# 1,450 products of zeros on TensorE ahead of an attention and feed-forward kernel

## The chip, the cores and the metric

The kernel runs on one core of one Trainium2 chip. The metric is the device time of one execution in microseconds. A core has five engines with queues of their own: TensorE (PE, with its loads of the stationary operand shown apart as PEld), VectorE (DVE), ScalarE (ACT), GpSimd (POOL) and SyncE (SP). Each works through its queue in order; waits between the queues are semaphores, which the framework puts in from the tiles that an instruction reads and writes.

## The reference

Attention in chunks of 32 tokens over 16 tokens to the left, 8 to the right and 8 memory entries, for 4 x 8 heads of 64, and then a feed-forward layer of 512 to 2048 to 512 over all 3,072 tokens:

```python
for c in range(nc):                       # nc = 768 // 32
    q_c = q[:, :, c_start:c_end]
    k_full = np.concatenate([mem_k, k[:, :, l_start:r_end]], axis=2)
    v_full = np.concatenate([mem_v, v[:, :, l_start:r_end]], axis=2)
    scores = scale * np.matmul(q_c, k_full.transpose(0, 1, 3, 2))
    scores = scores - np.max(scores, axis=-1, keepdims=True)
    a = np.exp(scores)
    a = a / (np.sum(a, axis=-1, keepdims=True) + 1e-09)
    out[:, :, c_start:c_end] = np.matmul(a, v_full)
...
h = x @ w_in
g = np.where(h >= 1, h, np.where(h <= -1, 0.0, (h + 1) ** 2 / 4.0))
return (g @ w_out).astype(np.float32)
```

## The kernel before

The 3,072 tokens are cut into 6 blocks of 512 (TB). A block's attention is made in two halves of 256 tokens: scores on TensorE (pe_scores, first_attention), maximum, difference and sum on VectorE, the exponential on ScalarE, transposition, and the product with the values (pe_values). Its result goes into the tiles xth and xtl: every float32 operand of the feed-forward layer is kept as a high part of the type float32r and a low part, the rest.

The feed-forward layer has 16 steps a block (NFC), one for each 128 of the 2048 columns. In a step pe_hidden makes 12 products of 128x128 by 128x512 into the tile ps_h (high by high, low by high, high by low, for four pieces of 128 rows), ScalarE and VectorE work out the gate and its parts gh and gl, and pe_out makes 12 more into the four banks of ps_o. In 96 steps these are 2,304 products of full size, less what the early steps do in halves of 256 columns.

The weights come from memory in 16 pieces w_0 to w_15 of 8,192 bytes a partition. Each piece is turned in place into its high and low part by decode: one pass on ScalarE, three on VectorE, one on ScalarE, one on VectorE. Decodes, the attention of the first three blocks and the first 32 feed-forward steps are interleaved by the list FIRST, in which a name stands for the next part of its chain and "+" for the next load of the list early. After it the loop over s goes on step by step.

Every engine's instructions are kept in the order of the program (the class InOrder). So VectorE and ScalarE can't pass a step that waits for TensorE, and SP can't issue a load ahead of one that waits. SP's first loads are, in this order: query and key tiles 0 and 1 (first_qk), value tile 0 (first_v), w_0, value tile 1, query tile 2, w_1, query tile 3, value tiles 2 and 3, w_2 and so on.

At the start stand the memset of the tile warm on VectorE, keep_warm(8), which is eight products of warm with itself that nobody reads, and make_identity, which writes ident on GpSimd. Then the list begins with the scores of the first attention (g0).

Memory: the pool const has ident (512 bytes a partition) and the 16 weight tags; xpool, apool and gpool follow. In order of first use const's tags are ident, w_0, w_13 (borrowed first by query tile 2), w_1, w_14 (query tile 3), w_15 (value tiles 2 and 3), w_2, w_3, w_4, w_5 and the rest. Query tiles 0 and 1 and value tiles 0 and 1 are in apool. Together the tiles of all pools take about 222 KB of a partition. All operands of the large products start at multiples of 512 bytes from one another: the pieces of the weights and of xth and xtl by their sizes, gh and gl through the 128 bytes of the tile "offset" ahead of them.

Of the kernel before, what the change touches and what calls it, by code (L numbers as in the profile page):

```python
# [8 lines left out]
F32 = mybir.dt.float32  # L9
F32R = mybir.dt.float32r  # L10
# [6 lines left out]
P = 128  # L17
# [34 lines left out]
LAST = 2  # L52


class InOrder:


# [3 lines left out]
    def __getattr__(self, name):  # L61
        def call(*args, **kwargs):
            return self.tc.keep_in_program_order(getattr(self.engine, name)(*args, **kwargs))  # L63

        return call


@with_exitstack
def attn_ffn_kernel(ctx: ExitStack, tc: tile.TileContext, first_qk, first_v, qk, vw, w, out):
    nc = tc.nc  # L70
    engines = (nc.tensor, nc.scalar, nc.vector, nc.gpsimd, nc.sync)
    pe, act, dve, pool, sp = (InOrder(tc, e) for e in engines)
# [8 lines left out]
    SEQ = 24  # L81
    SCALE = 1.0 / float(D) ** 0.5
    n2 = 2 * DM

    const = ctx.enter_context(tc.tile_pool(name="const", bufs=1))
    xpool = ctx.enter_context(tc.tile_pool(name="xpool", bufs=2))
# [43 lines left out]
    place = {key: divmod(n, 2) for n, key in enumerate(weight_order(NFC))}  # L130
# [421 lines left out]
    for name in FIRST.split():  # L552
# [4 lines left out]
        if name not in chains:  # L557
            kind, i = name[0], int(name[1:])
# [15 lines left out]
    for s in range(first * NFC, steps):  # L574
# [30 lines left out]
        else:  # L605
            n, i = LAST // LAG, s - first * NFC
# [11 lines left out]
def weight_order(n):  # L618

    order = [(0, 0), (0, 1)]  # L620
    for fc in range(2, n):
        order += [(0, fc), (1, fc - 2)]
    return order + [(1, n - 2), (1, n - 1)]
# [81 lines left out]
```

## Time and profile before

| | us |
|---|---|
| median of 2 runs | 599.89 |
| lowest, highest | 599.82, 599.96 |
| the profiled execution | 600.11 |
| its span, first to last instruction | 598.3 |
| ScalarE busy | 280.3 |
| VectorE busy | 325.6 |

The profile is that of one execution. "Busy" is the union of an engine's instructions; for TensorE the ends are modelled, so that consecutive products overlap in the rows and their spacing has to be read from starts. The mean granted clock of TensorE over the span is 0.999 of full speed. In rows of the timeline the first number is the start in us from the first instruction, the second how long the merged instructions last, "x8" their number, and the bracket the idle time of the engine before them with what ended it. In rows of groups the numbers behind the bar are busy time in us, mean duration of one in ns, and idle time before.

### The profile page before, as it was taken

How to read it: one execution, taken by the hardware profiler on the slowest of the kernel's cores; microseconds unless marked ns; L12 is line 12 of the kernel's file. 1: busy time of each engine (PE TensorE's matmuls, PEld its weight loads, DVE VectorE, ACT ScalarE, POOL GpSimd, SP SyncE). 2: the span in 40 equal slices, each digit the busy share in tenths (PEclk: the TensorE clock that was granted, in tenths of full speed). 3: DMA queues.
4: the chain of work that ended last, by engine and by line, in shares of the span. 5: the costliest groups of instructions: out<-in, count | busy, mean ns of one | idle time of the engine just before them, and what ended most of it. 6: DMA issues, size and time to landing. Idle time of an engine off the chain costs nothing.

```text
span 598.3 us, 12265 instructions
## 1 busy us (share of the span) xinstructions
PE 582.7 (97%) x5496; PEld 483.5 (81%) x5496; DVE 325.6 (54%) x466; ACT 280.3 (47%) x503; POOL 0.7 (0%) x6
## 2 busy tenths in 40 slices
PE   5899999999999999999999999999999999999996
PEld 2888888788888888888888888888888888888885
DVE  5999999986474224636423644623564632322222
ACT  2689864554435335444435443434443444543442
POOL 0000000000000000000000000000000000000000
PEclk9999999999999999999999999999999999999999
DMA  8999300424051004012101223200310000100001
GB/s 355 422 418 419 148 1 0 178 82 168 1 177 71 0 1 158 26 65 108 71 1 71 107 71 107 71 1 34 144 71 2 1 2 0 71 0 1 0 1 70
DMA packets 9844, 55.31 MB, mean 92 GB/s; under 512 B 1088, under 2 KB 1088, under 8 KB 5184
## 3 DMA queue, kind: packets, MB, share of 16 engines
q1 hardware_dynamic: 9792, 54.53, 23.6%
q8 instruction: 43, 0.70, 0.5%
q14 instruction: 9, 0.07, 0.0%
HBM read 48.23 MB, written 6.29 MB: 91 GB/s over the span
## 4 chain that ended last, share of the span: by engine, by line
PE 82%; DVE 15%; issue 2%; DMA 1%; ACT 0%; DVEq 0%; ACTq 0%
PE ps_o L63 38%; PE ps_h L63 38%; DVE f L63 6%; PE ps_x L63 3%; DVE wr L63 2%; PE ps_s L63 2%; DVE gw L63 1%; DVE gl L63 1%; DVE pr L63 1%; DVE den L63 1%; DMA qk<-in_first_qk_dram 1%; DVE pt L63 1%; DVE mx L63 1%; DVE xtl L63 0%; DVE rin L63 0%
## 5 line engine op out<-in xcount | busy, mean ns | idle before, releaser
L63 PE MATMUL ps_h<-xth,wr 128*128 128x512 f32 (+1 forms) x832 | 195.6, 377 | 1.1 <-DVE wr L63 1.1
L63 PE MATMUL ps_o<-wr,gh 128*128 128x512 f32 x768 | 194.7, 390 | 0.0
L63 PEld LDWEIGHTS ps_h<-xth,wr 128*128 128x128 f32 x832 | 149.0, 190 | 30.3 <-DVE wr L63 1.5
L63 PEld LDWEIGHTS ps_o<-wr,gh 128*128 128x128 f32 x768 | 143.3, 188 | 29.4
L63 DVE SCALAR_TENSOR_TENSOR gw<-gw,gt 128x512 f32<-128x512 f32 (+1 forms) x104 | 67.2, 649 | 164.9 <-ACT gw L63 164.6
L63 ACT ACTIVATE gw<-ps_h 128x512 f32<-128x512 f32 (+1 forms) x104 | 58.6, 563 | 159.0 <-PE ps_h L63 158.9
L63 PE MATMUL ps_o<-wr,gl 128*128 128x512 f32 x384 | 106.9, 389 | 0.0
L63 PE MATMUL ps_h<-xtl,wr 128*128 128x512 f32 (+1 forms) x416 | 104.8, 374 | 0.0
L63 DVE TENSOR_TENSOR gl<-gw,gh 128x512 fp32r<-128x512 f32 (+1 forms) x104 | 67.4, 649 | 65.8 <-ACT gh L63 65.7
L63 ACT CAST gh<-gw 128x512 fp32r<-128x512 f32 (+1 forms) x104 | 61.1, 590 | 69.9 <-DVE gw L63 69.9
L63 PEld LDWEIGHTS ps_h<-xtl,wr 128*128 128x128 f32 x416 | 75.3, 190 | 13.9
L63 PEld LDWEIGHTS ps_o<-wr,gl 128*128 128x128 f32 x384 | 72.1, 188 | 15.1
L63 ACT ACTIVATE gw<-gw 128x512 f32<-128x512 f32 (+1 forms) x104 | 62.4, 600 | 0.0
L63 ACT ACTIVATE gt<-ps_h 128x512 f32<-128x512 f32 (+1 forms) x104 | 58.3, 561 | 0.0
L63 DVE STREAM_TRANSPOSE pt<-pr 32x512 f32<-32x512 f32 (+1 forms) x60 | 41.2, 698 | 1.3
L63 DVE SCALAR_TENSOR_TENSOR f<-w,f 128x1024 uint32<-128x1024 uint32 x32 | 39.0, 1220 | 0.4
L63 ACT ACTIVATE pr<-pr 128x1024 f32<-128x1024 f32 (+1 forms) x14 | 13.1, 937 | 35.1 <-DVE pr L63 35.0
L63 PEld LDWEIGHTS ps_x<-pt,v 64*64 64x64 f32 x1536 | 25.1, 142 | 5.0 <-issue 3.3
L63 PE MATMUL ps_x<-pt,v 64*64 64x32 f32 x1536 | 26.6, 226 | 1.2 <-ACT pt L63 1.2
L63 ACT CAST xth<-ps_x 128x512 fp32r<-128x512 f32 x24 | 13.1, 591 | 20.6 <-PE ps_x L63 20.6
L63 ACT CAST wr<-f 128x1024 fp32r<-128x1024 f32 x16 | 16.8, 1051 | 11.7 <-DVE f L63 11.7
L63 PEld LDWEIGHTS ps_s<-qk 64*32 64x32 f32 x1536 | 17.1, 112 | 6.1 <-issue 3.1
(27 smaller groups left out, 182.6 us busy)
## 6 DMA issues: line engine op xcount, KB each, us to landing
w<-in_w_dram SPq DMA_DIRECT2D x16, 1024.0 KB, 19.8
qk<-in_qk_dram SPq DMA_DIRECT2D x10, 1536.0 KB, 6.5
v<-in_vw_dram SPq DMA_DIRECT2D x10, 1024.0 KB, 5.5
out_dram<-ob SPq DMA_DIRECT2D x24, 256.0 KB, 2.0
qk<-in_first_qk_dram SPq DMA_DIRECT2D x4, 768.0 KB, 8.7
v<-in_first_v_dram SPq DMA_DIRECT2D x4, 512.0 KB, 12.7
```

Of the source, the lines that this page charges most:

```text
L63: return self.tc.keep_in_program_order(getattr(self.engine, name)(*args, **kwargs))
```

## The change

Ahead of all pools a tile of zeros is made, 128 partitions by two halves of 8,704 float32r words (69,632 bytes a partition), and filled by one memset on VectorE (the half for stationary operands) and one on GpSimd (the half for moving operands). Then pe_zeros issues 1,450 products, all into two banks of PSUM that nothing reads, and both pools are closed. The main part of the kernel is as it was.

The products are 30 alike, with both operands at the beginning of their halves, and then ten each of 142 kinds by the list that ahead gives: (place in bytes, step of the stationary columns in words, moving operand as one run or as runs of so many words at such a step, moving columns, stationary columns). In that order: 64 places 4 bytes apart; steps 2, 4, 8, 16, 32, 62, 64 and 66 at four places each; six patterns of the moving operand in which every second run is skipped, with steps 16 and 64 of the stationary one, at two places each; one such pattern with a stationary operand in one run, at two places; 128, 256 and 384 moving columns at four places each; 32 and 64 stationary columns at four places each.

```diff
+REPEAT = 10
+
+
+def ahead():
+
+    todo = [(4 * n, 1, 1, 512, 128) for n in range(64)]
+    todo += [(r, k, 1, 512, 128) for k in (2, 4, 8, 16, 32, 62, 64, 66) for r in (0, 16, 64, 128)]
+    for run, step in ((1, 2), (2, 4), (4, 8), (8, 16), (16, 32), (32, 64)):
+        todo += [(4 * run * r, k, (run, step), 512, 128) for k in (16, 64) for r in (0, 1)]
+    todo += [(r, 1, (32, 64), 512, 128) for r in (0, 128)]
+    todo += [(r, 1, 1, n, 128) for n in (128, 256, 384) for r in (0, 64, 128, 192)]
+    todo += [(r, 1, 1, 512, n) for n in (32, 64) for r in (0, 64, 128, 192)]
+    return todo
...
+def pe_zeros(pe, to, zeros):
+
+    fixed, moving = zeros[:, 0], zeros[:, 1]
+    for _ in range(3 * REPEAT):
+        ps = to.tile([P, 512], F32, name="ps_z")
+        pe.matmul(ps, fixed[:, 0:P], moving[:, 0:512], start=True, stop=True)
+    for place, step, kind, n, m in ahead():
+        c = place // 4
+        a = fixed[:, c : c + (m - 1) * step + 1 : step]
+        if kind == 1:
+            b = moving[:, 0:n]
+        else:
+            run, k = kind
+            b = moving[:, 0 : n // run * k].rearrange("p (b q) -> p b q", q=k)[:, :, 0:run]
+        ps = to.tile([P, 512], F32, name="ps_z")
+        for _ in range(REPEAT):
+            pe.matmul(ps[0:m, 0:n], a, b, start=True, stop=True)
...
+    with tc.tile_pool(name="ahead", bufs=1) as at, tc.tile_pool(name="ps_a", bufs=2, space=bass.MemoryType.PSUM) as to:
+        zeros = at.tile([P, 2, 8192 + 512], F32R, name="zeros")
+        dve.memset(zeros[:, 0].bitcast(F32), 0.0)
+        pool.memset(zeros[:, 1].bitcast(F32), 0.0)
+        pe_zeros(pe, to, zeros)
```

## The prediction

> **What bounds the kernel now.** I read the page first (busy time, the slices, the chain that ended last), then the timeline of the first 40 us, the timeline of TensorE alone in the middle of the run, and the groups of instructions with their shapes kept apart.
>
> ```profile
> span 598.3 us, 12265 instructions
> PE 582.7 (97%) x5496; PEld 483.5 (81%) x5496; DVE 325.6 (54%) x466; ACT 280.3 (47%) x503; POOL 0.7 (0%) x6
> PE 82%; DVE 15%; issue 2%; DMA 1%; ACT 0%; DVEq 0%; ACTq 0%
> ...
> L63 PEld LDWEIGHTS ps_o<-wr,gh 128*128 128x128 f32 x768 | 143.3, 188 | 29.4
> ```
>
> TensorE is busy for 97% of the span and carries 82% of the chain; VectorE's 15% is the start, where weights are decoded. So whatever is put on TensorE's queue adds its own time, unless it falls into one of the few holes. Every product has a load of its stationary operand (5496 of both), and loads run beside products. What one product takes in the dense part is read from starts, since the ends are modelled:
>
> ```profile
> 400.81 1.98 PE L63 MATMUL ps_h<-xth,wr 128*128 128x512 f32 x8
> 402.62 1.07 PE L63 MATMUL ps_h<-xtl,wr 128*128 128x512 f32 x4
> 403.53 1.98 PE L63 MATMUL ps_o<-wr,gh 128*128 128x512 f32 x8
> 405.35 1.07 PE L63 MATMUL ps_o<-wr,gl 128*128 128x512 f32 x4
> 406.25 1.98 PE L63 MATMUL ps_h<-xth,wr 128*128 128x512 f32 x8
> ```
>
> From 400.81 to 403.53 us twelve products with 512 columns start, and twelve more until 406.25: 2.72 / 12 = 226.7 ns each, whichever tile is stationary. The rows of the start give the other prices:
>
> ```profile
> 0.27 0.10 POOL L691 MEMSET const-float32-1.0<- 128x1 f32 x1
> ...
> 0.73 0.20 POOL masks.py:197 MEMSET ident<- 128x128 f32 x1 [0.29 <-POOLq L691]
> ...
> 0.86 0.27 DVE L63 MEMSET warm<- 128x256 uint32 x1 [0.86 <-PEq L691]
> ...
> 1.19 3.59 PE L63 MATMUL ps_h<-warm 128*128 128x512 bf16 x8 [1.19 <-DVE warm L63]
> ...
> 2.11 0.67 SPq L63 DMA_DIRECT2D w<-in_w_dram  x1
> ...
> 4.97 1.19 PE L63 MATMUL ps_s<-qk 64*32 64x64 f32 x64 [0.19 <-DMA qk<-in_first_qk_dram]
> 6.23 0.11 DVE L63 MEMSET ps_s<- 32x64 f32 x1 [5.10 <-PE ps_s L63]
> 6.38 0.69 DVE L63 TENSOR_REDUCE mx<-ps_s 128x8 f32<-128x512 f32 x1
> ...
> 11.32 1.12 ACT L63 ACTIVATE w<-w 128x1024 f32<-128x1024 f32 x1
> ...
> 23.86 2.07 PE L63 MATMUL ps_h<-xth,wr 128*128 128x256 f32 x8
> ...
> 25.73 1.05 PE L63 MATMUL ps_h<-xtl,wr 128*128 128x256 f32 x4
> 26.58 1.35 PE L63 MATMUL ps_h<-xth,wr 128*128 128x256 f32 x8
> ...
> 30.84 0.46 PEld L63 LDWEIGHTS ps_h<-ident,pr 128*128 128x128 f32 x4
> ...
> 36.26 0.65 PE L63 MATMUL ps_h<-xtl,wr 128*128 128x256 f32 x4
> ...
> 36.74 1.12 PE L63 MATMUL ps_h<-xth,wr 128*128 128x256 f32 x8
> ```
>
> **The change, part by part.** Nothing is removed. Added are two memsets, one on VectorE and one on GpSimd, 1,450 products that wait for both, and a use of memory that others wait for.
>
> Count of the products: 30 at first; then ten each at 64 places (640), at 8 steps by 4 places (320), 24 with both operands stepped (240), 2 with the moving one alone (20), 12 with 128, 256 or 384 columns (120), 8 with 32 or 64 stationary columns (80). So 1,330 have 512 columns, and 40 each 384, 256 and 128.
>
> *Start of the products.* VectorE fills 8,704 words. Its 64 words take 0.11 us and 256 take 0.27: 0.83 ns a word, 7.3 us. If nothing of the 0.27 is fixed, it is 1.05 ns a word and 9.2 us. GpSimd takes 0.10 us for one word and 0.20 for 128, so 0.79 ns a word and 6.9 us, or at most 0.20 / 128 = 1.56 ns and 13.6 us. The two run beside each other from 0.3 to 0.9 us on. I take 8.5 us for the first product, between 8 and 14. The three loads that open the queue of SP (both first query tiles, the first value tile) lie outside the zeros and are hidden under this.
>
> *The products.* 512 columns: 1,330 x 226.7 ns = 301.5 us. 256 columns: four products start between 36.26 and 36.74 us, 120 ns each; 40 make 4.8 us. 384 columns: the middle of the two, 173.4 ns, 6.9 us. 128 columns: the four loads at 30.84 us last 0.46 us together, one of them 0.19 by the first group row above, so 90 ns apart; with 120 as upper end I take 95 ns, 3.8 us. Sum 317.0 us. The clock starts low: the eight products with the tile warm take (3.59 - 0.63) / 7 = 423 ns if one alone takes 0.63, and the 256-column ones go from 2.07 us for eight at 23.86 to 1.35 at 26.58, after about four us of work from the scores before them on. Four us at 423 instead of 227 ns lose 9.5 x 0.196 = 1.9 us. Last product out of the way at 8.5 + 317.0 + 1.9 = 327.4 us; call it T.
>
> What these rows don't show is any product whose operands are read at another place or step: worked out from the sizes of the tiles, all of the dense ones read both operands in one run, at addresses that agree within 512 bytes. The bounds for that: a load of 128 columns goes through in 90 ns and a product lasts 227, so a load that takes up to 227 / 90 = 2.5 times as long stays hidden. Nearest rows for a stepped read are the decode steps, which take every second word:
>
> ```profile
> L63 DVE SCALAR_TENSOR_TENSOR f<-w,f 128x1024 uint32<-128x1024 uint32 x32 | 39.0, 1220 | 0.4
> L63 DVE TENSOR_TENSOR wr<-f,wr 128x1024 fp32r<-128x1024 f32 x16 | 19.5, 1218 | 0.0
> L63 ACT ACTIVATE w<-w 128x1024 f32<-128x1024 f32 x16 | 18.4, 1166 | 1.2 <-DMA w<-in_w_dram 1.2
> L63 ACT CAST wr<-f 128x1024 fp32r<-128x1024 f32 x16 | 16.8, 1051 | 11.7 <-DVE f L63 11.7
> ```
>
> VectorE takes 1220 ns with one stepped source and 1218 without; ScalarE 1166 against 1051, 11% more. So I take nothing for steps, as the cover is 2.5 times and the nearest rows show 1.0 and 1.1. Without cover, with loads at three times their time (270 ns), the 520 products whose stationary operand steps by four words or more (seven of the eight steps, and the 24 pairs) lose 43 ns each, 23 us; at four times (360 ns) 133 ns, 69 us. For places I take nothing either; the upper end is that load and product can't read at the same time at half of the 64 places: 320 x 90 ns = 29 us. A gain is not excluded: 226.7 ns is 13 ns more than twice the step from 256 to 512 columns, 2 x (226.7 - 120) = 213.4. If that is what the change of the stationary tile costs and ten equal loads don't pay it, 1,330 x 13.3 = 17.7 us go.
>
> The Trainium skill, page "TensorE: Matmul & The Clock Gate", section "Back-to-back issue gap", gives an isolated spacing of 512 columns at full clock of N / 2.4 + 2.5 ns, about 216 ns. By that the 512-column products would take 287 us and the sum would be some 14 us less; the dense rows here show 226.7 with a load between any two, so I keep the row.
>
> The Trainium skill, page "Advanced Engine Details and Errata", section "SBUF Cachelines", speaks against the change: reads that hit another 16-byte line with each element pay a penalty. It does not say how much, and no row here shows it on TensorE; it is the second rival below.
>
> *After T.* The tile of zeros takes 69,632 bytes of a partition, and the pool is closed again. The tiles of const that come first in order of use lie on it: ident, w_0 to w_4, part of w_5, and the first query and value tiles that borrow the places of w_13 to w_15. So the load of w_0 waits for the last product, and with it everything behind it on SP's queue, which is all loads but the first three; the memset of ident on GpSimd waits too. At T, TensorE goes on with the eight warm products (at full clock now, 8 x 227 ns = 1.8 us) and the first scores, whose tile has been there for long. VectorE's first reduction comes 6.38 - 4.97 = 1.4 us after the scores start: T + 3.2, where it was 6.38. The load of w_0 is needed when its decode opens, at 11.32 before, T + 8.1 now. Loading took:
>
> ```profile
> GB/s 355 422 418 419 148 1 0 178 82 168 1 177 71 0 1 158 26 65 108 71 1 71 107 71 107 71 1 34 144 71 2 1 2 0 71 0 1 0 1 70
> ...
> out_dram<-ob SPq DMA_DIRECT2D x24, 256.0 KB, 2.0
> ```
>
> 1 MB at 420 GB/s is 2.5 us, plus at most the 2.0 that a small store takes from issue to landing: T + 5, in time by 3 us. The later loads start with 2 MB fewer ahead of them than before, so the chain of VectorE that follows is as it was. From the first reduction to the end there were 598.3 - 6.38 = 591.9 us. New span: T + 3.2 + 591.9 = 922.5 us. If the first three loads waited for T as well, the scores would start at about T + 4.2 and it would be 2.4 us more; if w_0 didn't wait, nothing changes, as VectorE's queue is held by the first scores.
>
> The profiled execution took 600.11 us with its span of 598.3, so 1.8 us lie around the span; the median of the runs shown, 599.89, is 0.2 under it. 922.5 + 1.8 - 0.2 = 924.1 us.
>
> **The rivals.** First, on the other side: the products don't reach the chip, since nothing reads what they write. Then only the memsets are left. The warm tile is filled behind the 7.3 us on VectorE, everything on TensorE moves from 1.19 to about 8.5 us, and at most those 7.3 us are added: 607 us, within 2%. It decides if fewer than some 20 products (12 us less 7.3, by 227 ns) are kept. Against it: the eight warm products are never read either, have the same operands, and all eight stand in the trace with a load each. Chance 0.02. Its half form, that of ten equal products one is kept, leaves 145: 9 + 33 us, about 640; chance 0.01.
>
> Second, steps cost: a stepped load takes four times as long, so that 520 products wait for theirs. 924 + 69 = 993 us. For it: nothing in the trace, which has no such load; against it the 1.0 and 1.1 above, though those step by two words only. It decides from 2.5 times on. The Trainium skill, page "Advanced Engine Details and Errata", section "SBUF Cachelines", would have it so for steps of four 4-byte elements or more, without a size. Chance 0.13.
>
> Third, places cost: load and product hold each other up where their addresses differ within 512 bytes. 924 + 29 = 953 us with half of the places hit. For it: all rows agree within 512 bytes, so none speaks. Chance 0.10.
>
> Fourth, the products are cheaper than the kernel's own, since the same stationary tile comes ten times: 924 - 18 = 906 us. Against it: the warm products, equal ones too, still show their loads. Chance 0.06.
>
> **How the numbers follow.** The forecast, all 1,450 products at the prices of the dense part, has 0.68, and its time is 924 us; its own range is 914 to 940, with the late memset (5.5 us), the first loads (2.4 us) and some ns for a stepped load upward, and a part of the 13 ns downward. The range with 8 in 10 goes from 905, just under the fourth rival, to 975, which holds the third and the case of loads at three times their time (947); left out are the second rival at four times and the two cases without products. Within 2% of before (588 to 612 us, about what a measurement of this kernel can tell from no change) lies only the first rival, 0.02; faster is given 0.01 for what I don't see; slower 0.97.
>
> **What would show it.** In the changed profile, right: a block of about 317 us on TensorE ahead of the warm products, with starts 226.7 ns apart, beginning between 8 and 14 us; after it the timeline of before, moved by the same amount to the end; the wait of SP at w_0 in that block. A second or third rival shows in the groups as another spacing for a step or a place, with starts of the loads apart by as much; the first one as missing products. Wrong would be the sum if the spacing in the plain places, the first 30, were not 227 ns; wrong would be the step after T if the first reduction came more than 5 us after the last product, or if VectorE's chain of decodes then waited for loads.

## The result and the profile after

The changed kernel takes 959.61 us (959.2 to 960.01), 1.60 times the time before (95% interval 1.593 to 1.607). The profiled execution took 960.01 us with a span of 958.2. Page of the changed kernel: the span, the busy times, the granted clock in 40 slices, and the groups of the new products.

```profile
span 958.2 us, 15170 instructions
PE 932.6 (97%) x6945; PEld 779.7 (81%) x6946; DVE 333.2 (35%) x467; ACT 280.6 (29%) x503; POOL 8.1 (1%) x7
...
PEclk9999999999999996899999999999999999999999
...
L78 PE MATMUL ps_z<-zeros 128*128 128x512 f32 (+5 forms) x1450 | 349.6, 404 | 10.1 <-DVE zeros L78 10.1
L78 PEld LDWEIGHTS ps_z<-zeros 128*128 128x128 f32 (+2 forms) x1450 | 294.2, 229 | 64.9 <-issue 17.6
```

All 1,450 products are there, each with its load. They are busy for 349.6 us, where 319 were forecast, and the idle time ahead of them is 10.1 us, not 8.5. The rest of TensorE's work is the same (the busy time grew by 349.9). The granted clock has a dent in the slices behind the products, which the section on the hole takes up.

The products are told apart by their order in the list. Busy time of the tile zeros in stretches that begin and end where the kinds change; columns are the stretch, its length, the engines' busy times with their counts, and the granted clock:

```profile
core 0: us, PE busy (x) PEld busy (x) DVE busy (x) POOL busy (x), PEclk, DMA share, GB/s
20.11:168.69 148.58, 148.58 (x641) 120.39 (x641) 0.00 (x0) 0.00 (x0) 1.00 0.00 1
168.69:245.28 76.59, 76.59 (x321) 75.13 (x320) 0.00 (x0) 0.00 (x0) 1.00 0.00 1
245.28:281.77 36.49, 36.49 (x81) 24.30 (x81) 0.00 (x0) 0.00 (x0) 1.00 0.00 0
281.77:320.07 38.30, 38.30 (x162) 38.25 (x160) 0.00 (x0) 0.00 (x0) 1.00 0.00 1
320.07:341.02 20.95, 20.95 (x141) 19.89 (x140) 0.00 (x0) 0.00 (x0) 1.00 0.00 1
341.02:359.40 18.38, 18.38 (x81) 9.62 (x79) 0.00 (x0) 0.00 (x0) 1.00 0.00 0
```

Length by the number of products gives the spacing (a count is one or two higher where a neighbour overlaps the edge): 640 places 232.2 ns, 320 steps of the stationary operand 239.3, the 80 with moving runs of one or two words 456.1, the 160 with longer runs 239.4, the 80 with few stationary columns 229.8. In the third row the loads are busy for two thirds of the time only, so those products don't wait for loads; in the second and fourth row loads are busy for 98% of the time and more.

What follows the products, in the timeline of the changed kernel:

```profile
359.74 0.33 SPq L78 DMA_DIRECT2D w<-in_w_dram  x1
359.77 0.20 POOL masks.py:197 MEMSET ident<- 128x128 f32 x1 [351.69 <-PE ps_z L78]
...
362.61 0.69 DVE L78 TENSOR_REDUCE mx<-ps_s 128x8 f32<-128x512 f32 x1
...
372.06 2.98 PE L78 MATMUL ps_x<-pt,v 64*64 64x32 f32 x99
...
377.21 1.07 PE L78 MATMUL ps_x<-pt,v 64*64 64x32 f32 x29 [2.18 <-issue]
```

The load of w_0 and the memset of ident wait until the last product is through, as worked out. VectorE's first reduction stands at 362.61 us; from there to the end it is 958.2 - 362.61 = 595.6 us, where 591.9 were forecast. The last row has a hole that was not there before: TensorE sits idle for 2.18 us in the middle of 128 products with the values, and no instruction in the profile ends it.

So 35.7 us lie between forecast and profiled execution (960.01 against 924.3 on its own basis): 1.6 at the start, 30.4 in the products, 3.7 behind them.

### The profile page after: what moved, and what is told of

It reads as the page before. It is cut to its first block, busy times and chain, and to the rows that moved or that the text cites. A ratio compares the mean times of both kernels' runs of the same rounds, so it can differ in the third digit from the quotient of the medians.

```text
span 958.2 us, 15170 instructions
## 1 busy us (share of the span) xinstructions
PE 932.6 (97%) x6945; PEld 779.7 (81%) x6946; DVE 333.2 (35%) x467; ACT 280.6 (29%) x503; POOL 8.1 (1%) x7
## 4 chain that ended last, share of the span: by engine, by line
PE 89%; DVE 8%; issue 2%; ACT 1%; DVEq 0%; ACTq 0%
PE ps_z L78 36%; PE ps_o L78 24%; PE ps_h L78 24%; DVE f L78 3%; PE ps_x L78 2%; PE ps_s L78 2%; DVE wr L78 1%; DVE gw L78 1%; DVE zeros L78 1%; DVE gl L78 1%; DVE pr L78 0%; DVE pt L78 0%; DVE mx L78 0%; DVE den L78 0%; ACT gw L78 0%
## 5 line engine op out<-in xcount | busy, mean ns | idle before, releaser
L78 PE MATMUL ps_z<-zeros 128*128 128x512 f32 (+5 forms) x1450 | 349.6, 404 | 10.1 <-DVE zeros L78 10.1
L78 PEld LDWEIGHTS ps_z<-zeros 128*128 128x128 f32 (+2 forms) x1450 | 294.2, 229 | 64.9 <-issue 17.6
```

## The experiments

Eleven kernels, in the order of the questions. In those that have other products than the change, only the products of zeros differ and the main part is whole.

### The same products at one place

```diff
-    for place, step, kind, n, m in ahead():
-        c = place // 4
+    for _, _, _, n, m in ahead():
+        c, step, kind = 0, 1, 1
```

> The same 1,450 products with the same numbers of columns, but all at place 0, in one run and with no step. Theory: the 1,300 of 512 columns behind the first 30 go at 226.7 ns, the last one is through at about 331 us, the main part is as late as in the changed kernel (595.6 us from its first reduction): 931 us. What is left to 924 is then the later start, the waits of the first 30 and the main part. Rival (zeros or waits cost 5 ns at any place): 938 us.

Measured 930.24 us (ratio to before 1.551, 1.548 to 1.553). The first reduction stands at 334.39 us. The stretch behind the first 30 products, busy times of the tile zeros:

```profile
20.10:331.20 311.10, 311.10 (x1421) 254.74 (x1419) 0.00 (x0) 0.00 (x0) 1.00 0.00 1
```

The theory holds for the products: the 1,220 of full size in this stretch start 226.7 ns apart, only the 80 with 32 or 64 stationary columns come at 230 to 232. Zeros as such, or ten equal stationary tiles in a row, cost and save nothing. The same stretch of the changed kernel takes 359.4 - 20.1 = 339.3 us, so place, step and run together cost 28.2 us. The two profiled executions differ by 30.1 us (960.01 against 929.92); the other 1.9 lie in the main part, which took 593.7 us from its first reduction here and not the 595.6 that were expected.

### Which moving patterns cost

```diff
+    ("run1of2", 0, 1, 2, 512, 1, 128),
...
+    ("run1of4", 0, 1, 4, 512, 1, 128),
...
+    ("run4of8at2", 2, 4, 8, 512, 1, 128),
...
+    for name, at, run, k, n, step, m in KINDS:
+        a = fixed[:, 0 : (m - 1) * step + 1 : step]
+        b = moving[:, at : at + n // run * k].rearrange("p (b q) -> p b q", q=k)[:, :, 0:run]
+        ps = to.tile([P, 512], F32, name="ps_" + name, tag="z")
+        for _ in range(COUNT):
+            pe.matmul(ps[0:m, 0:n], a, b, start=True, stop=True)
```

> In place of the 1,450 products: 30 plain ones, then 40 each of eleven moving patterns with a plain stationary operand, one tile of PSUM for each pattern. Theory (pieces): TensorE takes its moving operand from memory in pieces of 16 bytes, four words, about 1.78 ns each (455 ns for the 256 pieces of the slow patterns), and a product lasts as long as the larger of 512 words and its pieces. Spacing in ns: plain and plain from word 1 about 227 to 232; runs 1 of 2 and 2 of 4: 455; 4 of 8: 232; 1 of 4 and 1 of 8: 910; 2 of 8: 455; 6 of 8 with 504 columns (168 pieces): 299; 4 of 8 from word 2 (256 pieces): 455; 8 of 16 from word 2 (192 pieces): 341. Rival (short runs): a run of less than four words halves the rate whatever its step or place: 1 of 4, 1 of 8 and 2 of 8 at 455, and the three patterns with longer runs at 232. Rival (both stepped): only a moving step together with a stationary step costs, so all at 227 to 232.

Timeline of TensorE in this kernel; names end where a trailing number is left out, and the second row of 1 and 2 words are the steps of 8 and, for one word, of 4 and 8 together. The spacing is the difference of consecutive starts by 40:

```profile
19.14 9.23 PE L79 MATMUL ps_plain<-zeros 128*128 128x512 f32 x40
28.20 18.29 PE L79 MATMUL ps_run1of<-zeros 128*128 128x512 f32 x40
46.31 18.31 PE L79 MATMUL ps_run2of<-zeros 128*128 128x512 f32 x40
64.45 9.51 PE L79 MATMUL ps_run4of<-zeros 128*128 128x512 f32 x40
73.80 35.86 PE L79 MATMUL ps_run1of<-zeros 128*128 128x512 f32 x80
109.47 18.59 PE L79 MATMUL ps_run2of<-zeros 128*128 128x512 f32 x40
127.87 12.06 PE L79 MATMUL ps_run6of<-zeros 128*128 128x504 f32 x40
139.75 18.22 PE L79 MATMUL ps_run4of8at<-zeros 128*128 128x512 f32 x40
157.79 13.25 PE L79 MATMUL ps_run8of16at<-zeros 128*128 128x512 f32 x40
170.86 9.65 PE L79 MATMUL ps_plainat<-zeros 128*128 128x512 f32 x40
```

Plain 226.5 ns; one of two and two of four 453; four of eight 234; one of four 461 and one of eight 431 (not 910); two of eight 460; six of eight 297; four of eight from word 2 on 451; eight of sixteen from word 2 on 327; plain from word 1 on 237, by single starts. The rival of both operands stepped falls, since the stationary one is plain here. The rival of short runs falls by the row at 139.75: the same runs of four words double when they begin two words into a 16-byte piece. My own theory falls in part: if each piece took 1.78 ns, one word of four would be at 910, and it stands at 461, next to the 453 of one of two. What fits these rows best is a price by the word: four words that fill a piece go at the full rate, all others at half of it, about 0.88 ns each. It is a fit and not exact: for eight of sixteen from word 2 on it gives 340 ns, and 327 were found. All of this holds for words of four bytes; no other type was run.

### What the runs cost in the changed kernel

```diff
-        if kind == 1:
+        if kind == 1 or kind[0] < 4:
```

> The changed kernel, but the eight kinds whose moving operand comes in runs of one or two words read it in one run instead; their stationary operand stays stepped by 16 or 64 words. Theory: their 80 products fall from 456 to about 238 ns, so 17 to 18 us less, 942 us, and nothing else moves. Rival (stationary step at fault in these kinds): 959 to 960 us.

Measured 940.78 us (ratio 1.568, 1.566 to 1.571), 18.8 us less. The 80 products, on the same steps of the stationary operand, now take 18.6 us instead of 36.5:

```profile
245.28:263.90 18.62, 18.62 (x81) 18.62 (x81) 0.00 (x0) 0.00 (x0) 1.00 0.00 0
```

So 17.9 us are theirs. Most of the other 0.9 lies in the main part, which took 594.5 us from its first reduction here instead of 595.6.

### Which stationary steps cost

```diff
+    ("by1", 0, 128, 128, 128, 1, 128),
...
+    ("by8", 0, 128, 128, 128, 8, 128),
...
+    ("by64", 0, 128, 128, 128, 64, 128),
```

> In place of the 1,450 products: 30 plain ones, then 40 each with the stationary columns at another step, all but the last with only 128 moving columns in one run, so that the load sets the spacing. Theory (pieces): a load takes the larger of 0.87 ns a column and 1.78 ns a piece of 16 bytes. Spacing in ns: steps 1 and 2: 112 to 115; step 3 (96 pieces): 171; steps 4, 16, 32, 64: 226 to 235; steps 8, 62, 66 somewhat more, 250 to 260, as their loads last 25 to 35 ns longer in the changed kernel; 64 columns at step 8: 114 to 125, 32 columns at step 8: about 60; step 8 with 512 moving columns: 244. Rival (later, not slower): a stepped load starts its data later but passes as many columns a second, so all steps stay at 112 and the 233 to 249 ns of the changed kernel come from somewhere else.

With 128 moving columns the load sets the spacing. Stretches of this kernel for steps 1, 2, 4, 8 and 66, 40 products each (stretch, length, busy times of PE, PEld and the three other engines, granted clock):

```profile
18.46:22.88 4.42, 4.42 (x42) 4.41 (x40) 0.00 (x0) 0.00 (x0) 0.00 (x0) 1.00 0.00 0
22.88:27.60 4.72, 4.72 (x43) 4.72 (x42) 0.00 (x0) 0.00 (x0) 0.00 (x0) 1.00 0.02 3
35.50:44.80 9.30, 9.30 (x41) 9.30 (x42) 0.00 (x0) 0.00 (x0) 0.00 (x0) 0.50 0.00 0
44.82:54.40 9.58, 9.58 (x41) 9.58 (x42) 0.00 (x0) 0.00 (x0) 0.00 (x0) 0.50 0.01 2
...
90.77:100.60 9.83, 9.83 (x41) 9.83 (x42) 0.00 (x0) 0.00 (x0) 0.00 (x0) 0.50 0.00 0
```

These are 111, 118, 233, 240 and 246 ns; steps 16, 32 and 64 came at 220 to 223 and step 62 at 243. So a load whose columns step by four words or more takes twice its time, 2.0 to 2.2 times. Steps 8, 62 and 66 are the worst, as expected, but at 240 to 246 ns and not 250 to 260. The rival (later, not slower) falls. Step 3 came at some 200 ns, not 171; at step 8, 64 columns came at 121 and 32 at 63 ns, as expected.

The clock of 0.50 in three of the rows was not expected: TensorE's rows fill the stretch, yet the clock is halved while it waits for loads. It does not set these spacings: step 8 with 512 moving columns, at full clock at the end of the block, comes at 244 ns, and so does step 8 in the changed kernel. It does set one: 64 columns at step 1 come at 107 ns, a quarter of the 427 ns that 512 moving columns take at half the clock (the first ten products of the changed kernel), so that row says nothing of the load.

### Why the plain places cost 5 ns

```diff
+    for n in range(COUNT):
+        if n % 10 == 0:
+            ps = to.tile([P, 512], F32, name="ps_tens", tag="z")
+        pe.matmul(ps, fixed[:, 0:P], b, start=True, stop=True)
...
+    ps = to.tile([P, 512], F32, name="ps_places", tag="z")
+    for n in range(COUNT):
+        c = n // 10
+        pe.matmul(ps, fixed[:, c : c + P], b, start=True, stop=True)
```

> In place of the 1,450 products: 30 plain ones and then 300 each of five kinds, all with 128 and 512 columns in one run: at place 0 with a new tile of PSUM after every ten; at place 0 in one tile; with four stationary pieces in turn; at place 0 as sums of twelve; at 30 places one word apart in one tile. Theory (places): the 231 to 233 ns of the plain products come from stationary addresses that differ from the moving ones: the first four kinds at 227, the places at 232. Rival (waits): each new tile makes its first product wait on TensorE's own counter, which disturbs the spacing: tens at 231 to 233, the other four at 227. Rival (zeros alone): operands that stay the same or the lack of other work cost 5 ns: all five at 232.

Timeline of TensorE, 300 products a row:

```profile
19.03 68.16 PE L66 MATMUL ps_tens<-zeros 128*128 128x512 f32 x300
87.03 68.16 PE L66 MATMUL ps_one<-zeros 128*128 128x512 f32 x300
155.03 68.16 PE L66 MATMUL ps_turns<-zeros 128*128 128x512 f32 x300
223.03 68.16 PE L66 MATMUL ps_sums<-zeros 128*128 128x512 f32 x300
291.03 69.84 PE L66 MATMUL ps_places<-zeros 128*128 128x512 f32 x300
360.93 1.89 PE L66 MATMUL ps_h<-warm 128*128 128x512 bf16 x8
```

The first four kinds start 68.00 us apart, 226.7 ns a product; the 30 places take 232 to 233 (69.9 us until the warm products). So it is the places, and neither the waits nor the zeros.

### Which places, and the half pieces again

```diff
+    ("f16m0x", 16, 0, 512, 512),
...
+    ("f64m0x", 64, 0, 512, 512),
...
+    ("f16m16x", 16, 16, 512, 512),
...
+    ("run4of6at0x", 0, 0, 4, 6),
```

> In place of the 1,450 products 30 plain ones and 40 each of 22 kinds. First stationary operand at word 4, 16, 32, 64, 96, 128 with the moving one at 0; then moving at 4, 16, 32, 64, 128 with stationary at 0; then both at word 1, 4, 16, 32, 64. Theory (difference): what counts is the difference of the two addresses within 512 bytes: 226.7 ns at 128 words and wherever both move alike, 230 to 237 elsewhere. Rival (own place): each operand's own address counts, so that both at 4, 16 or 32 are as slow as one. Then moving patterns, runs of words at a step from a word on. Theory (word by word): a piece of 16 bytes of which all four words are wanted takes 1.78 ns, any other takes 0.88 ns a word: 2 of 4 from word 1 and from word 3 and 2 of 8 from word 2 at 452 ns, 16 of 32 from word 2 at 282, from word 0 at 232, 4 of 6 at 340. Rival (pieces at 1.78 ns, whatever is taken of them, at most 455 in all): 2 of 4 from word 1 and 2 of 8 from word 2 at 455, 2 of 4 from word 3 at 455, 16 of 32 from word 2 (160 pieces) at 284, 4 of 6 (192 pieces) at 341.

The name has the first word of the stationary (f) and of the moving operand (m):

```profile
27.72 9.49 PE L89 MATMUL ps_f16m0x<-zeros 128*128 128x512 f32 x40
37.05 9.47 PE L89 MATMUL ps_f32m0x<-zeros 128*128 128x512 f32 x40
46.36 9.25 PE L89 MATMUL ps_f64m0x<-zeros 128*128 128x512 f32 x40
55.44 9.47 PE L89 MATMUL ps_f96m0x<-zeros 128*128 128x512 f32 x40
64.74 9.26 PE L89 MATMUL ps_f128m0x<-zeros 128*128 128x512 f32 x40
...
119.69 9.67 PE L89 MATMUL ps_f1m1x<-zeros 128*128 128x512 f32 x40
129.20 9.37 PE L89 MATMUL ps_f4m4x<-zeros 128*128 128x512 f32 x40
138.41 9.24 PE L89 MATMUL ps_f16m16x<-zeros 128*128 128x512 f32 x40
147.49 9.28 PE L89 MATMUL ps_f32m32x<-zeros 128*128 128x512 f32 x40
```

A stationary operand 16 words away costs (233 ns), both moved by 16 words cost nothing (227), nor does a difference of 64 words (227), while 96 costs (232). So the difference counts in the main, within 256 bytes and not 512. The rule is not whole: both moved by one word come at 238 ns, where the moving operand no longer begins with a whole piece, and both by four words at 230, while the stationary one alone moved by four words costs nothing (227); the moving one alone costs 5 ns at four words and only 2 at 16. The moving patterns can't decide between the two theories of this run: two of four from word 1 and word 3 at 453, two of eight 460, four of six 340 as both say, and 16 of 32 from word 2 at 298, 5% above both. From word 0 the same runs come at 240 and not 232, though nothing is stepped but the moving operand.

### The places in the kernel itself

Without the 128-byte tile "offset" gh and gl, stationary for all products into ps_o, lie 128 bytes off the weights:

```diff
-    gpool.tile([P, 32], F32, name="offset", bufs=1)
```

> The kernel before the change without its 128-byte tile offset, so that gh and gl, the stationary operands of the 1,152 products into ps_o, begin 128 bytes away from the weights within 512 bytes; nothing else changes, and the output is the same. Theory (difference of the addresses): these products go at 232 to 236 ns instead of 226.7, 6 to 10 us more, 606 to 610 us; those into ps_h stay at 226.7. Rival: the 5 ns of the places belong to the products of zeros alone: 599.9 us.

Measured 608.16 us (ratio to before 1.0135, 1.0118 to 1.0152), 8.2 us more: a small cost, but clear of the noise and on the theory's side. Timeline of TensorE in the dense part:

```profile
405.14 2.01 PE L63 MATMUL ps_h<-xth,wr 128*128 128x512 f32 x8
...
407.90 2.03 PE L63 MATMUL ps_o<-wr,gh 128*128 128x512 f32 x8
...
410.70 2.01 PE L63 MATMUL ps_h<-xth,wr 128*128 128x512 f32 x8
```

Twelve products into ps_o take 2.80 us, 233 ns each instead of 226.7. Those into ps_h were expected to stay and don't: 2.76 us, 230 ns. By the starts of single products, the first seven behind ps_o come 236, 224, 231, 236, 228, 233 and 230 ns apart and the next four at 226 to 227: whatever the two reads do to each other outlasts the change of operands.

With 256 bytes of difference instead:

```diff
-    gpool.tile([P, 32], F32, name="offset", bufs=1)
+    gpool.tile([P, 96], F32, name="offset", bufs=1)
```

> The kernel before the change with the tile offset at 384 bytes in place of 128, so that gh and gl begin 256 bytes away from the weights within 512 bytes. Theory (difference within 256 bytes, as 64 words either way cost nothing in the products of zeros): the products into ps_o stay at 226.7 ns, 600 us. Rival (within 512 bytes): 606 to 610 us as without the tile.

Measured 599.95 us, ratio 1.0002 (0.9992 to 1.0011): no cost, so here too a difference of 256 bytes counts as none.

### The hole behind the products

```diff
-    for _ in range(3 * REPEAT):
-        ps = to.tile([P, 512], F32, name="ps_z")
-        pe.matmul(ps, fixed[:, 0:P], moving[:, 0:512], start=True, stop=True)
...
-        for _ in range(REPEAT):
+        for _ in range(REPEAT - (place in (4, 8, 12) and m == 128 and n == 512 and step == 1 and kind == 1) * 4):
```

> The changed kernel without the first 30 products and with four fewer at each of three places, 42 products and 84 instructions less, so that the blocks of 256 instructions in which TensorE's program is loaded begin at the same instructions of the main part as before the change. By the products alone: 10.8 us less (42 at 231 ns and 1.1 us of waits for new tiles), 948.8 us. Theory (late block): the hole of 2.2 us in the products with the values, ended by nothing the profile shows, is a block that comes too late, and with the blocks as before it and what follows go: from the first reduction to the end 591.9 us instead of 595.6, in all 945.1 us. Rival: the loads that all start at once are at fault, and the hole stays: 948.8 us.

Measured 945.87 us (ratio 1.576, 1.573 to 1.579). From the first reduction at 352.27 to the end of the span, 944.2, it is 591.9 us, and the products with the values run through:

```profile
361.71 3.64 PE L78 MATMUL ps_x<-pt,v 64*64 64x32 f32 x128
```

In the kernels with other numbers of products such holes stand at other instructions, but always at the same place within 256: counted through TensorE's products and loads, the instruction behind the hole has the remainder 192 to 194 in every kernel that has one, and the part from the first reduction on takes 591.9 to 598.9 us. The instruction queue of the DMA shows the blocks themselves: the page of the changed kernel has 54 of its packets, of 16 KB each, 11 more than before for 2,900 more instructions of TensorE, and by the trace one of them runs from 374.65 to 375.75 us, across the start of the hole; in the other kernels, too, one starts 2.4 to 2.6 us before a hole ends. So the 3.7 us are no matter of the loads that start at once: they depend on where in the main part a block of the program begins.

The hole itself is only part of them. In the changed kernel VectorE's first subtraction from ps_x stands 16.34 us behind the first reduction instead of 15.04, so 1.3 us of the 2.18 get through. The other 2.3 come later, from a second stretch at half the clock. First the changed kernel, then the one with both memsets on GpSimd (see the next section), which puts the same instructions on TensorE (columns as in the experiment on stationary steps):

```profile
390.30:397.00 6.70, 6.70 (x81) 6.05 (x78) 5.94 (x9) 2.14 (x4) 0.00 (x0) 0.50 1.01 418
```

```profile
396.30:403.00 6.70, 6.67 (x103) 6.19 (x104) 6.70 (x11) 3.92 (x9) 0.00 (x0) 1.00 1.01 418
```

At half the clock four products into ps_o take 1.87 us until the next start, where they take 1.03 in the kernel with 42 products fewer. The GpSimd kernel has a longer hole (3.47 us) and no such stretch, and its main part takes 593.8 us; three other kernels with one hole among these 128 products have 3.4 us at half the clock instead of 6.8, and take 593.7 to 594.5. With the hole gone the stretch was gone too, but a hole doesn't always bring it: why the clock fell here the runs don't show.

### The late memset

Both halves of the zeros on VectorE, and both on GpSimd:

```diff
-        pool.memset(zeros[:, 1].bitcast(F32), 0.0)
+        dve.memset(zeros[:, 1].bitcast(F32), 0.0)
```

> The changed kernel with both halves of the zeros filled on VectorE, one after the other. Theory (GpSimd in the way): VectorE's first memset began at 2.62 us, and not at 0.86 as the small one did, because GpSimd's was under way; alone it begins at 0.86, the first product at 15.6 us. Rival (the large memset itself begins late): at 2.62 us again, the first product at 17.4 us.

```diff
-        dve.memset(zeros[:, 0].bitcast(F32), 0.0)
+        pool.memset(zeros[:, 0].bitcast(F32), 0.0)
```

> The changed kernel with both halves of the zeros filled on GpSimd, one after the other, and only the tile warm on VectorE. Theory (GpSimd in the way): the memset of warm begins later than 0.86 us, near 2.6 us; the first product at 15.5 us. Rival (the large memset itself begins late): warm at 0.86 us.

969.35 and 963.67 us, one run each. VectorE alone, in the timeline of the first of the two kernels:

```profile
2.62 7.31 DVE L78 MEMSET zeros<- 128x8704 f32 x1 [2.62 <-issue]
11.69 7.31 DVE L78 MEMSET zeros<- 128x8704 f32 x1 [1.76 <-issue]
19.01 0.27 DVE L78 MEMSET warm<- 128x256 uint32 x1
```

The theory falls: without GpSimd the large memset begins at 2.62 us again, and the second 1.76 us after the first, while the small one follows at once. In the second kernel GpSimd's two run without a gap and warm begins at 0.86 us. So a memset of this size on VectorE has 1.76 us ahead of it that the profile does not show as busy; why, these runs don't say.

## Why the prediction was right and wrong

The direction and the order of size came from the right step: products on a queue that is busy for 97% of the span add their own time, at the spacing of the dense part. That spacing, 226.7 ns, holds to the tenth for products of zeros at one place, and all at one place the kernel comes at 930 us, 6 us above the forecast of 924.1. That nothing reads the products, and that ten equal loads follow each other, changed nothing, so the first and the fourth rival fall.

The step that failed is the one on what the rows don't show: "I take nothing for steps" and "For places I take nothing either". In its terms:

- The moving runs had no term at all. The 320 + 240 + 20 stepped products were counted, but only the load of the stationary operand was bounded. The 80 with runs of one or two words took 36.5 us instead of 18.1, 18.4 us more, half of the miss, and plain runs in their place gave 17.9 of it back. That the load rows of this stretch are idle a third of the time shows that the hidden load was the wrong operand to ask about.
- The cover for a stepped load was sized at 2.5 times (227 / 90). The load goes through in 111 ns, not 90, so the cover was 2.0, and steps of four words or more take 2.0 to 2.2 times. So the second rival had the mechanism, and "it decides from 2.5 times on" had the wrong edge. It cost 4.0 us in the 320, and not 69. The 160 with longer runs cost 2.0 more, but there the two operands can't be told apart: runs of 4 and 16 words with a plain stationary operand come at 234 and 240 ns by themselves. The Trainium skill, page "Advanced Engine Details and Errata", section "SBUF Cachelines", has the penalty for a new 16-byte line with each element, and the loads agree; it also has two hits on a line as enough, and the moving operand disagrees: two of the four words of a piece come at 453 ns, and there the measurement decides.
- Places cost 5.5 ns in 640 products, 3.5 us. That is the third rival, again with its mechanism (the difference of the addresses) and a size far too large (29 us).
- The first 30 took 10.0 us, not 8.7. Each has a tile of its own out of two, so that it waits for an earlier product: the profile shows their loads idle until one ends, and at full clock they start 324 and 236 ns apart in turn, about 1.0 us in all. With one tile for all 30 (the kernel of the moving patterns) they take 19.14 - 10.07 = 9.1 us, and 8.4 to 9.0 in the three others that do so. That products never wait on their own engine was assumed without being said.
- Products with 128 columns came at 111 ns, not 95: with the 20 that have a stepped moving operand alone 0.9 us. Those with 32 or 64 stationary columns add 0.2.

At the start, 0.83 ns a word for VectorE's memset was right (7.31 us for 8,704 words); its beginning at 0.86 us was not: it began 1.76 us later. After T everything went as worked out up to the first reduction: the loads behind w_0 waited, were in time, and 3.2 us passed until the reduction. What was wrong is "the chain of VectorE that follows is as it was": 3.7 us, 1.3 from a block of instructions that came too late for 128 short products and 2.3 from half the clock behind it, both gone with the blocks at their old places. Nothing in the argument spoke of where the program's blocks fall, although 2,900 instructions were put ahead.

The sum of these, 1.6 + 1.3 + 3.5 + 4.0 + 18.4 + 2.0 + 0.9 + 0.2 + 3.7, is 35.6 us, against 35.7 found. The measured time lies outside the forecast's own range of 914 to 940. It lies in the range of 905 to 975 by luck: the upper end was kept for the third rival and for slow loads, which together took 7.5 to 9.5 us, and the moving runs, which filled half of the miss, stood in no term and no rival.

## What to carry to other kernels

Price both operands of a product, not only the one that is hidden: a moving operand of float32r words that doesn't come in whole, aligned groups of four costs up to twice the time, and a stationary one that steps by four words or more uses up a cover of two. Look at where operands lie with respect to each other: 128 bytes of padding that no line of code reads are worth 8 us in this kernel. When many instructions are put ahead of a stretch of very short ones, the stretch itself can change by some us with nothing in it changed.

## What the runs showed of the hardware that was not expected

- The granted clock fell to 0.50 while TensorE's rows were without a gap, in the stretches where products of 128 columns waited for loads of 200 to 246 ns (0.50 from 30.4 to 105.4 us in the kernel of the stationary steps). By the Trainium skill, page "TensorE: Matmul & The Clock Gate", "Part 1: The HAM clock gate", the clock follows how busy the array has been; that agrees if waiting for a load does not count as work, which no run here tests by itself.
- Products whose two operands lie a multiple of 256 bytes apart settle at 226.7 ns, most others keep moving between 224 and 241 (the kernel without the tile offset), and there it takes some seven products to settle again.
- The eight warm products, in bfloat16 and each with its own load, start 215 to 216 ns apart at full clock in the changed kernel, and the float32r products 226.7. So a load between two products does not by itself cost the 11 ns.
- A memset of 8,704 words on VectorE begins 1.76 us after it could, twice in a row; the same on GpSimd does not.
- 128 short products in 3.6 us use up a block of 256 instructions of TensorE; in eight of the kernels the next one came late among them, and TensorE stood still for 1.8 to 3.5 us.
